# One run of score matmuls for each second-half head, over three banks of PSUM

## The chip, the cores and the metric

The kernel runs on one core of one Trainium2 chip. The metric is the device time of one execution in microseconds (us), as the median of several runs. The engines are TensorE (PE in the profile; its weight loads are PEld), VectorE (DVE), ScalarE (ACT), GpSimd (POOL) and SyncE (SP), which issues all the DMAs of this kernel.

## What is computed

A decayed causal attention over 4 batches of 8 heads, 576 positions and 64 dimensions each, and behind it a mixture of four two-layer experts over the 2304 rows that come out.

```python
scores = q @ k.T / sqrt(D) + (cum[:, None] - cum[None, :])   # cum: running sum of log f
scores = where(causal, -1e9, scores); scores -= max(scores)
attn = exp(scores); attn /= attn.sum() + 1e-9
x = (attn @ v) -> [2304, 512]
for e in range(4):
    out += p[:, e] * (relu(x @ w1[e]) @ w2[e])                # p: normalized domain_probs
```

## The kernel before, in words

A number is held as two parts, a high one and the rest (hi and lo), and a product is three matmuls, or two where one operand carries both parts. The rows of a batch are cut into a first half (queries 0 to 255) and a second half (256 to 575); a job is a pair of heads of one batch and one half, so there are 16 jobs and 32 heads of the second half. This document counts these heads from 0 to 31; the first head of a job is even (`hh` 0), the second odd.

A second-half head has three tiles of 128 queries, tiles 2, 3 and 4, which start at query 256, 384 and 448 (`TOK0`; tile 4 overlaps tile 3 by 64) and see 384, 512 and 576 keys. `qk_pe` (line 600) makes the scores of a tile with two fp32 matmuls for each piece, the first with the high parts (`s<-hi` in the profile), the second with the rests and the decay rows (`s<-kl,q`). A piece is at most one bank of PSUM, 512 columns; tile 4 is cut into two of 288, which take a bank each. `qk_min` (628) adds the mask and takes the minimum of the negated scores on VectorE, out of PSUM into the tile `p`. `qk_exp` (644) does the exponential and its sum on ScalarE. `qk_tile` (656) calls the three in turn for one tile. Behind a head's three tiles `recip16` (673) takes the reciprocals of the sums, and `turn16` (694) splits the probabilities into the two fp16 parts `z` (ScalarE and VectorE) and has SP issue a transposing DMA of each tile into `pt` (726). `av_pair` (806) multiplies a job's `pt` by v for both heads, 28 matmuls into one bank, and `out16` (869) copies the result to its chunk of x on ScalarE. The banks of `ps_a` (four, line 107) hold the scores, the product, and some small transposes.

Interleaved with it, all the time, run the experts: a `Step` (997) has 24 matmuls of the first layer (`l1`, line 1013), a gate on ScalarE and VectorE (1026, 1027), 12 matmuls of the second layer (`l2`, 1046), and every second step a gather of its two output banks on VectorE (`acc`, 1068 and 1073). The weights stream in through SP.

What sets the order: `head_steps` (888) writes for each head a list of small steps with a cost each; `pace` (1552) walks the list so that the sum of costs goes up in a straight line with the experts' steps, in eighths of a step, towards the points at which a chunk of x has to be there, and the end. In this list a second-half head is its tiles (cost `TOK0[t] + 328`: 584, 712, 776), `recip16` and `turn16` at no cost. In an odd head `av_pair` of the job before (cost 1000), `out16` and the steps that make a finished chunk ready stand behind the second entry (line 913). In the first two heads the end of the first half's last job stands behind the first entry (line 919). The order of the list is a priority: within it the framework's planner, which times the kernel by a model, writes down for each engine what it finds ready, and each engine then runs its own order strictly.

Of the kernel before, what the change touches and what calls it, by code (L numbers as in the profile page):

```python
# [8 lines left out]
F32 = mybir.dt.float32  # L9
# [15 lines left out]
TOK0 = (0, 128, 256, 384, 448)  # L25
# [54 lines left out]
def fused(ctx: ExitStack, tc: tile.TileContext, qk, v, f, probs, w, out):  # L80
    nc = tc.nc
# [25 lines left out]
    ps_a = PS("ps_a", 4)  # L107
# [5 lines left out]
    q2 = [once_p.tile([66, S - CH], F32R, name=f"q2_{hh}") for hh in range(2)]  # L113
# [380 lines left out]
    class Job:  # L494
# [96 lines left out]
        def begin(self, hh):  # L591
# [3 lines left out]
            if hh == 0:  # L595
                n = len(self.its)
                self.ssum = st_p.tile([128, 2, n], F32, tag="ssum", name=f"ss{self.nm}")
                self.rs = st_p.tile([128, 2, n], F32, tag="rs", name=f"rs{self.nm}")

        def qk_pe(self, hh, its):  # L600

            at = 512
            for t in its:
                o = self.qo + TOK0[t] - self.q0
                w_ = TOK0[t] + 128
                cuts = ((0, w_),) if w_ <= 512 else ((0, w_ // 2), (w_ // 2, w_))
                for n, (a, z) in enumerate(cuts):
                    if at + z - a > 512:
                        ps = ps_a.tile([128, 512], F32, tag="a", name=f"s{self.nm}_{hh}_{t}_{n}")
                        at = 0  # L610
                    i = TOK0[t] - self.q0
                    for m, (lhsT, rhs) in enumerate(
                        (
                            (self.hi[hh][:, o : o + 128], self.hi[hh][:, self.ko + a : self.ko + z]),
                            (q2[hh][:, i : i + 128], self.kl[hh][:66, a:z]),
                        )
                    ):
                        nc.tensor.matmul(  # L618
                            out=ps[:, at : at + z - a],
                            lhsT=lhsT,  # L620
                            rhs=rhs,
                            start=(m == 0),
                            stop=(m == 1),
                        )
                    self.sp.setdefault((hh, t), []).append((a, z, ps[:, at : at + z - a]))
                    at += z - a

        def qk_min(self, hh, t):
            pt, nm, col = self.p[hh, t], self.nmax[hh], 2 * (t - self.its[0])
# [258 lines left out]
    def head_steps(n):  # L888
# [4 lines left out]
        if n + 1 < len(heads):  # L893
            j, hh = heads[n + 1]
            st.append((0, lambda j=j, hh=hh: j.prep(hh)))
        if n + 2 < len(heads):
            j, hh = heads[n + 2]
            st.append((0, lambda j=j, hh=hh: j.far(hh)))
            st.append((0, lambda j=j, hh=hh: j.load(hh)))
        qs, ts, us = [], [], []  # L900
        if n < len(heads):
            j, hh = heads[n]
            for t in j.its:
                qs.append((TOK0[t] + 328, lambda j=j, hh=hh, t=t: j.qk_tile(hh, t)))
            if j.half:
                qs.append((0, lambda j=j, hh=hh: j.recip16(hh)))
                for t in j.its:
                    qs.append((0, lambda j=j, hh=hh, t=t: j.turn16(hh, t)))
            elif hh == 1:
                qs.append((0, j.recip))  # L910
        if n - 2 >= FIRST and heads[n - 2][1] == 1 and heads[n - 2][0].half:
            j = heads[n - 2][0]
            qs[2:2] = [(1000, j.av_pair), (0, j.out16)] + ready(n - 2)
        if n - 2 >= FIRST and heads[n - 2][0].half == 0:
            j, hh = heads[n - 2]
            late_ = [(200, lambda j=j, hh=hh: j.av(hh))]
# [3 lines left out]
        if FIRST < n <= len(heads):  # L920
            j, hh = heads[n - 1]
            for gi in range(len(j.blocks())):
                ts.append((500, lambda j=j, hh=hh, gi=gi: j.tr(hh, gi)))
        if n + 1 < len(heads):
            j, hh = heads[n + 1]
# [572 lines left out]
    def ready(n):  # L1498
        return [(0, c) for c in sorted(done_at) if done_at[c] == n]
# [3 lines left out]
    for n in range(FIRST, len(heads) + 2):  # L1503
        for cost_, f_ in head_steps(n):
            if type(f_) is int:
                if f_ < LAST[0]:
                    asteps.extend(turn(f_))
                need[f_] = len(asteps)
            else:
                asteps.append((cost_, f_))  # L1510
# [20 lines left out]
    at = 0  # L1531
# [82 lines left out]
    j = heads[FIRST][0]  # L1614
# [159 lines left out]
```

## Time and profile before

| | us |
|---|---|
| median of 3 runs (924.88 to 925.85) | 925.6 |
| the profiled execution | 930.58 |
| span of its instructions | 928.8 |
| TensorE busy in it | 882.4 |
| VectorE busy | 710.0 |
| ScalarE busy | 569.3 |
| GpSimd busy | 528.0 |

The granted TensorE clock was 0.991 of full speed over the span. In the profile an engine is busy from the start of an instruction to its modelled end; matmuls overlap, so the time that one costs is read from the start of one to the start of the next. L618 is line 618. A wait names what ended it.

### The profile page before, as it was taken

What the parts mean: (1) busy time and instruction counts of PE and PEld (TensorE: products, weight loads), DVE (VectorE), ACT (ScalarE), POOL (GpSimd) and SP (SyncE); (2) the same over time, 40 slices, a digit from 0 to 9 for tenths busy, and PEclk for the clock granted to TensorE, in tenths of its full rate; (3) what the DMA queues carried; (4) which work ended last, traced back from release to release, by engine and by line L of the source; (5) the groups of instructions that cost most, each with busy time, mean ns of one, the idle gap of its engine ahead of it and who ended that gap; (6) DMA issues with size and microseconds to landing.
All of it is one profiled execution on the core that took longest, in us unless ns stands there. A gap on an engine that the chain in (4) does not pass through costs nothing.

```text
span 928.8 us, 16629 instructions
## 1 busy us (share of the span) xinstructions
PE 882.4 (95%) x5783; PEld 620.7 (67%) x5783; DVE 710.0 (76%) x1458; ACT 569.3 (61%) x1137; POOL 528.0 (57%) x528
## 2 busy tenths in 40 slices
PE   4899989998998899999999999899998999999998
PEld 3699879898876567666666666554455654666547
DVE  5768766686998888799888887676678647786487
ACT  5868766557676567767767775555665345653350
POOL 4655675655555552455635673785778527885060
PEclk9999989999999999999999999999999999999999
DMA  7457755455979969889999996744323324232003
GB/s 266 144 165 260 260 176 151 159 166 166 262 186 220 283 166 246 219 168 255 265 261 214 262 229 167 246 172 148 115 69 103 125 68 136 68 116 67 23 1 92
DMA packets 147508, 159.45 MB, mean 172 GB/s; under 512 B 86148, under 2 KB 107328, under 8 KB 147424
## 3 DMA queue, kind: packets, MB, share of 16 engines
q1 hardware_dynamic: 147424, 158.39, 61.1%
q8 instruction: 45, 0.74, 0.3%
q14 instruction: 39, 0.32, 0.1%
HBM read 117.30 MB, written 21.65 MB: 150 GB/s over the span
## 4 chain that ended last, share of the span: by engine, by line
PE 55%; POOL 12%; DVE 10%; ACT 7%; DMA 7%; issue 4%; SPq 0%; ACTq 0%; POOLq 0%; DVEq 0%
PE l L1046 16%; PE l L1013 15%; PE y L1284 8%; PE m L1284 7%; PE s L618 4%; POOL s L1344 4%; POOL wt L1178 3%; PE o L818 2%; POOL wu L1178 1%; DMA wr<-in_w 1%; DMA pk<-in_w 1%; DVE acc L1073 1%; DVE z L717 1%; DMA vr<-in_v 1%; ACT wt L1205 1%
## 5 line engine op out<-in xcount | busy, mean ns | idle before, releaser
L1013 PE MATMUL l<-y,w 128*128 128x256 f16 x1248 | 154.8, 275 | 2.7 <-ACT w L980 1.9
L647 ACT ACTIVATE p<-p,nm 128x576 f32<-128x576 f32 (+3 forms) x160 | 95.7, 599 | 82.7 <-DVE nm L632 77.9
L1013 PEld LDWEIGHTS <-w 128*128 128x128 f16 x1248 | 118.4, 99 | 34.2 <-issue 7.1
L1046 PE MATMUL l<-w,gh 128*128 128x512 f16 x408 | 122.2, 382 | 2.7 <-DVE acc L1073 2.0
L564 POOL CAST q<-raw 64x320 fp32r<-64x320 f32 (+1 forms) x56 | 28.1, 502 | 149.6 <-PE s L618 148.2
L1073 DVE SCALAR_TENSOR_TENSOR acc<-y,scg,acc 128x256 f32<-128x256 f32 (+1 forms) x164 | 81.1, 515 | 14.9 <-PE y L1284 14.7
L717 DVE SCALAR_TENSOR_TENSOR z<-p,rs,z 128x384 f16<-128x384 f32 (+3 forms) x128 | 82.4, 665 | 12.7 <-ACT z L716 11.3
L1284 PE MATMUL m<-rh,bs 128*128 128x512 f16 x256 | 86.6, 379 | 0.0
L572 POOL TENSOR_TENSOR kl<-raw,hi 64x576 fp32r<-64x576 f32 (+1 forms) x56 | 66.5, 1188 | 33.8 <-ACT hi L563 28.3
L618 PE MATMUL s<-hi 128*128 128x384 f32 (+1 forms) x192 | 74.9, 394 | 11.3 <-DVE hi L578 8.9
L632 DVE CUSTOM_DVE_ANT_0 p<-s,mask 128x288 f32<-128x288 f32 (+2 forms) x160 | 74.4, 473 | 13.3 <-PE s L618 12.7
L1210 POOL TENSOR_TENSOR bs<-wt,bs 128x512 f16<-128x512 f32 x32 | 38.1, 1192 | 71.3 <-ACT bs L1209 71.1
L1046 PE MATMUL l<-w,gl 128*128 128x512 f16 x204 | 77.3, 382 | 0.0
L716 ACT ACTIVATE z<-p,rs 128x384 f16<-128x384 f32 (+3 forms) x128 | 69.4, 589 | 7.0 <-DVE rs L678 3.4
L1027 DVE SCALAR_TENSOR_TENSOR gl<-l,gh 128x512 f16<-128x512 f32 (+1 forms) x80 | 54.8, 685 | 16.5 <-ACT gh L1026 15.8
L1013 PE MATMUL l<-xh,wh 128*128 128x256 f32 x224 | 65.1, 293 | 0.9 <-ACT xh L859 0.9
L957 POOL TENSOR_TENSOR wl<-wr,wh 128x512 fp32r<-128x512 f32 x48 | 61.7, 1313 | 7.3 <-ACT wh L953 3.6
L1284 PE MATMUL m<-rh,bw 128*128 128x512 f16 x191 | 64.4, 379 | 1.4 <-ACT r L1330 1.4
L1013 PE MATMUL l<-xl,wh 128*128 128x256 f32 x224 | 65.3, 292 | 0.0
L618 PE MATMUL s<-kl,q 66*128 66x384 f32 (+1 forms) x192 | 63.2, 334 | 2.2 <-DMA kl<-nc 2.2
L1013 PE MATMUL l<-xh,wl 128*128 128x256 f32 x224 | 65.2, 292 | 0.1
L1284 PEld LDWEIGHTS <-bs 128*128 128x128 f16 x384 | 37.6, 98 | 38.4
(385 smaller groups left out, 2344.0 us busy)
## 6 DMA issues: line engine op xcount, KB each, us to landing
wr<-in_w SPq DMA_DIRECT2D x90, 512.0 KB
pk<-in_w SPq DMA_DIRECT2D x64, 256.0 KB
wd<-w SPq DMA_DIRECT2D x32, 512.0 KB
raw<-in_qk SPq DMA_DIRECT2D x32, 448.0 KB
bw<-wd SPq DMA_DIRECT2D x32, 256.0 KB
bv<-wd SPq DMA_DIRECT2D x32, 256.0 KB
raw<-in_qk SPq DMA_DIRECT2D x24, 256.0 KB
vp<-in_v SPq DMA_DIRECT2D x10, 512.0 KB
```

The lines of the kernel that those rows point to most:

```text
L572: eng.tensor_tensor(out=kl[:64, :wk], in0=r[:64, ko : ko + wk], in1=hi[:64, ko : ko + wk].bitcast(F32), op=ALU.subtract,)
L618: nc.tensor.matmul(out=ps[:, at : at + z - a], lhsT=lhsT, rhs=rhs, start=(m == 0), stop=(m == 1),)
L632: nc.vector.tensor_tensor_reduce(out=pt[:, a:z], in0=ps, in1=mask[:, m0 + a : m0 + z], scale=-0.125, scalar=BIG if n == 0 else nm[:, col : ...
L647: nc.scalar.activation(out=pt[:, :w_], in_=pt[:, :w_], func=AF.Exp, scale=-1.0, bias=self.nmax[hh][:, c : c + 1], accum_out=self.ssum[:, h ...
L716: nc.scalar.activation(out=o[:, 0], in_=x, func=AF.Copy, scale=sc)
L717: nc.vector.scalar_tensor_tensor(out=o[:, 1], in0=x, scalar=sc, in1=o[:, 0], op0=ALU.mult, op1=ALU.subtract)
L957: eng.tensor_tensor(out=wl[n][:, a:z], in0=r[:, a:z], in1=wh[n][:, a:z].bitcast(F32), op=ALU.subtract,)
L1013: nc.tensor.matmul(out=self.l1p[:, fi, :], lhsT=lhsT, rhs=rhs[:, k, :], start=(k == 0 and m == 0), stop=(k == 3 and m == 2),)
L1027: self.last = nc.vector.scalar_tensor_tensor(out=self.gl, in0=self.l1p, scalar=0.0, in1=self.gh.bitcast(F32) if wide else self.gh, op0=ALU ...
L1046: matmul(out=l2[tt], lhsT=lhsT, rhs=rhs, start=(self.ps == 0 and fi == 0 and m == 0), stop=(self.ps == 1 and fi == 1 and m == 2),)
L1073: nc.vector.scalar_tensor_tensor(out=acc[c][:, tt, d0:d1], in0=ps, scalar=sc, in1=acc[c][:, tt, d0:d1], op0=ALU.mult, op1=ALU.add,)
L1284: line.append(nc.tensor.matmul(**args))
```

## The change

All score matmuls of a second-half head are issued in one run (`qk_head`), ahead of its minima and exponentials: tile 2 and the last 128 keys of tile 4 share a bank, tile 3 has one, the first 448 keys of tile 4 have the third. In the list of steps the run has cost 1400 and each tile's minimum and exponential 224. `av_pair` and what follows it now stand behind the third entry of the list, so behind the run and the minima and exponentials of tiles 2 and 3. For the first half's heads `qk_pe` is written in another way and issues what it did.

```diff
--- before.py
+++ after.py
@@ -597,33 +597,38 @@
                 self.ssum = st_p.tile([128, 2, n], F32, tag="ssum", name=f"ss{self.nm}")
                 self.rs = st_p.tile([128, 2, n], F32, tag="rs", name=f"rs{self.nm}")
 
+        def qk_bank(self, hh, t):
+            return ps_a.tile([128, 512], F32, tag="a", name=f"s{self.nm}_{hh}_{t}")
+
+        def qk_piece(self, hh, t, a, z, ps):
+
+            o, i = self.qo + TOK0[t] - self.q0, TOK0[t] - self.q0
+            for m, (lhsT, rhs) in enumerate(
+                (
+                    (self.hi[hh][:, o : o + 128], self.hi[hh][:, self.ko + a : self.ko + z]),
+                    (q2[hh][:, i : i + 128], self.kl[hh][:66, a:z]),
+                )
+            ):
+                nc.tensor.matmul(out=ps, lhsT=lhsT, rhs=rhs, start=(m == 0), stop=(m == 1))
+            self.sp.setdefault((hh, t), []).append((a, z, ps))
+
         def qk_pe(self, hh, its):
 
             at = 512
             for t in its:
-                o = self.qo + TOK0[t] - self.q0
                 w_ = TOK0[t] + 128
-                cuts = ((0, w_),) if w_ <= 512 else ((0, w_ // 2), (w_ // 2, w_))
-                for n, (a, z) in enumerate(cuts):
-                    if at + z - a > 512:
-                        ps = ps_a.tile([128, 512], F32, tag="a", name=f"s{self.nm}_{hh}_{t}_{n}")
-                        at = 0
-                    i = TOK0[t] - self.q0
-                    for m, (lhsT, rhs) in enumerate(
-                        (
-                            (self.hi[hh][:, o : o + 128], self.hi[hh][:, self.ko + a : self.ko + z]),
-                            (q2[hh][:, i : i + 128], self.kl[hh][:66, a:z]),
-                        )
-                    ):
-                        nc.tensor.matmul(
-                            out=ps[:, at : at + z - a],
-                            lhsT=lhsT,
-                            rhs=rhs,
-                            start=(m == 0),
-                            stop=(m == 1),
-                        )
-                    self.sp.setdefault((hh, t), []).append((a, z, ps[:, at : at + z - a]))
-                    at += z - a
+                if at + w_ > 512:
+                    ps, at = self.qk_bank(hh, t), 0
+                self.qk_piece(hh, t, 0, w_, ps[:, at : at + w_])
+                at += w_
+
+        def qk_head(self, hh):
+
+            two, three, four = (self.qk_bank(hh, t) for t in (2, 3, 4))
+            self.qk_piece(hh, 2, 0, 384, two[:, :384])
+            self.qk_piece(hh, 4, 448, 576, two[:, 384:])
+            self.qk_piece(hh, 3, 0, 512, three)
+            self.qk_piece(hh, 4, 0, 448, four[:, :448])
 
         def qk_min(self, hh, t):
             pt, nm, col = self.p[hh, t], self.nmax[hh], 2 * (t - self.its[0])
@@ -900,8 +905,13 @@
         qs, ts, us = [], [], []
         if n < len(heads):
             j, hh = heads[n]
+            if j.half:
+                qs.append((1400, lambda j=j, hh=hh: j.qk_head(hh)))
             for t in j.its:
-                qs.append((TOK0[t] + 328, lambda j=j, hh=hh, t=t: j.qk_tile(hh, t)))
+                if j.half:
+                    qs.append((224, lambda j=j, hh=hh, t=t: (j.qk_min(hh, t), j.qk_exp(hh, t))))
+                else:
+                    qs.append((TOK0[t] + 328, lambda j=j, hh=hh, t=t: j.qk_tile(hh, t)))
             if j.half:
                 qs.append((0, lambda j=j, hh=hh: j.recip16(hh)))
                 for t in j.its:
@@ -910,7 +920,7 @@
                 qs.append((0, j.recip))
         if n - 2 >= FIRST and heads[n - 2][1] == 1 and heads[n - 2][0].half:
             j = heads[n - 2][0]
-            qs[2:2] = [(1000, j.av_pair), (0, j.out16)] + ready(n - 2)
+            qs[3:3] = [(1000, j.av_pair), (0, j.out16)] + ready(n - 2)
         if n - 2 >= FIRST and heads[n - 2][0].half == 0:
             j, hh = heads[n - 2]
             late_ = [(200, lambda j=j, hh=hh: j.av(hh))]
```

## Rows read from the trace of the kernel before

**Rows 1.** The page, part 1: busy us (share of span) xinstructions

```profile
PE 882.4 (95%) x5783; PEld 620.7 (67%) x5783; DVE 710.0 (76%) x1458; ACT 569.3 (61%) x1137; POOL 528.0 (57%) x528
```

**Rows 2.** Stretches: us, PE, PEld, DVE, ACT, POOL busy, PEclk, DMA share, GB/s

```profile
300.00:325.00 25.00, 22.08 (x156) 14.96 (x154) 21.97 (x48) 15.42 (x33) 12.83 (x13) 0.96 1.08 277
325.00:350.00 25.00, 25.00 (x178) 16.36 (x177) 21.51 (x50) 16.83 (x35) 12.51 (x12) 0.97 0.68 164
...
450.00:475.00 25.00, 25.00 (x185) 17.15 (x184) 21.82 (x50) 17.01 (x36) 13.65 (x12) 1.00 1.08 275
```

**Rows 3.** TensorE's waits: us in total, times, longest

```profile
PE o L818 <- DMA pt<-z: 5.0, 2, 2.7
...
PE l L1046 <- DVE acc L1073: 2.0, 2, 1.6
```

**Rows 4.** TensorE by time: start, us, what [idle before <-releaser]; av_pair's waits

```profile
296.75 1.69 PE L818 MATMUL o<-pt,v 128*64 128x320 f16 x27 [2.75 <-DMA pt<-z]
...
322.14 2.17 PE L818 MATMUL o<-pt,v 128*64 128x320 f16 x27 [2.23 <-DMA pt<-z]
```

**Rows 5.** TensorE by time: runs of tiles 4 and 3, starts of 2

```profile
441.71 0.52 PE L618 MATMUL s<-hi 128*128 128x384 f32 x1
...
447.09 0.38 PE L1046 MATMUL l<-w,gl 128*128 128x512 f16 x1
...
447.84 0.61 PE L1046 MATMUL l<-w,gh 128*128 128x512 f16 x2
...
452.57 0.38 PE L1046 MATMUL l<-w,gl 128*128 128x512 f16 x1
...
453.25 0.61 PE L1046 MATMUL l<-w,gh 128*128 128x512 f16 x2
...
463.30 0.42 PE L618 MATMUL s<-hi 128*128 128x384 f32 x1
```

**Rows 6.** TensorE by time: a pair of 128 columns, first half

```profile
60.76 0.28 PE L1013 MATMUL l<-xl,wh 128*128 128x256 f32 x1
...
61.35 0.22 PE L618 MATMUL s<-hi 128*128 128x128 f32 x1
...
61.69 0.28 PE L1013 MATMUL l<-xl,wh 128*128 128x256 f32 x1
```

**Rows 7.** SP's waits, two transposes on SP, POOL's waits (235 to 575)

```profile
SPq L538 <- PE s L618: 32.0, 21, 6.5
...
288.74 4.57 SPq L726 DMA_TRANSPOSE pt<-z  x2
...
POOL q L564 <- PE s L618: 105.5, 21, 11.0
```

**Rows 8.** VectorE by time, around the end of head 20

```profile
452.24 0.55 DVE L632 CUSTOM_DVE_ANT_0 p<-s,mask 128x384 f32<-128x384 f32 x1
...
453.26 0.43 DVE L675 TENSOR_SCALAR ss<-ss 128x3 f32<-128x3 f32 x1 [0.46 <-ACT p L647]
...
454.58 1.36 DVE L717 SCALAR_TENSOR_TENSOR z<-p,rs,z 128x384 f16<-128x384 f32 x2 [0.68 <-ACT z L716]
```

**Rows 9.** TensorE and VectorE by time: tile 4 of heads 1, 8, 18

```profile
231.40 0.44 PE L618 MATMUL s<-hi 128*128 128x288 f32 x1
...
239.50 0.50 DVE L632 CUSTOM_DVE_ANT_0 p<-s,mask,nm 128x288 f32<-128x288 f32 x1
...
308.81 0.38 PE L618 MATMUL s<-hi 128*128 128x288 f32 x1
...
316.00 0.46 DVE L632 CUSTOM_DVE_ANT_0 p<-s,mask 128x288 f32<-128x288 f32 x1
...
318.73 0.51 DVE L632 CUSTOM_DVE_ANT_0 p<-s,mask,nm 128x288 f32<-128x288 f32 x1
...
425.74 0.38 PE L618 MATMUL s<-hi 128*128 128x288 f32 x1
...
432.12 0.50 DVE L632 CUSTOM_DVE_ANT_0 p<-s,mask,nm 128x288 f32<-128x288 f32 x1
```

## The prediction

> **What bounds the kernel now.** I read the page's busy shares first, then the table of stretches, then TensorE's own waits, then the order on TensorE and VectorE around the scores. The page says that TensorE (PE) is busy for 882.4 of 928.8 us [rows 1]. The second-half heads run through the middle of the span. In its stretches TensorE is full (25.00 of 25 at 450 to 475) or short by a hole that can be named (22.08 at 300 to 325) [rows 2], so whatever adds TensorE time there adds to the end, and whatever closes a hole takes from it. VectorE is busy for about 22 of 25 us there: the second engine in line, not the bound. TensorE's waits in the stage are few [rows 3]: two for the transposed probabilities that the attention-times-v product reads (5.0 us), two for the gather on VectorE (2.0 us in the list). The two big ones stand in the order of time in [rows 4]: 2.75 us before 296.75 and 2.23 us before 322.14, both on the DMA that writes pt. After the second the granted clock falls: 0.96 and 0.97 of full in two stretches that would otherwise show 1.00 [rows 2].
>
> **The change part by part.**
>
> *The matmuls of the scores.* Columns stay at 2944 a head (twice 384, 512 and 576), and matmuls at 8. Three runs become one, and tile 4 is cut into 448 and 128 columns, not 288 and 288. What a run costs above its columns is read from starts, at 2.4 columns a ns. Tile 3: from the fp16 matmul at 452.57 to the next fp16 one at 453.25 is 0.68 us for 512 + 2x512 columns, which are 0.640: 0.040 above. Tile 4: 447.09 to 447.84 is 0.75 for 512 + 4x288, which are 0.693: 0.057 above [rows 5]. Tile 2 also has two matmuls, so it gets 0.040. That is 0.137 us a head. Two runs of 2 and 4 matmuls give 0.0085 us for each matmul and 0.023 for each run. After, six wide matmuls in one run are 0.023 + 6x0.0085 = 0.074.
>
> The two 128-column ones have no row in this stage, but first-half heads have such a pair. From 61.35 to 61.69 a pair of 128 and one of 256 take 0.34 us; 256-column matmuls around them follow each other every 0.118 (60.76 to 61.35 in five steps); so the pair takes 0.222, where its columns are 0.107: 0.115 above [rows 6]. So after is 0.189, and 0.052 more a head: x32 = **+1.7 us**. Bounds: if the narrow pair costs no more than two wide ones (0.017), the term is -1.5; if the run saves nothing (three times 0.023), it is +3.1. I take +1.7, since the narrow rows are of the same operation and the same kind of operands.
>
> [...]
>
> *The place of the attention-times-v product (av_pair).* The list of small steps is paced by its costs. A second-half head costs 584 + 712 + 776 = 2072 before and 1400 + 3x224 = 2072 after, so the pace, which hangs on the list's total and on a chunk that is due before these heads, doesn't change; a pair of heads with its product is 5144 and takes 21.6 us, from one pair's tile 2 at 441.71 to the next one's at 463.30 [rows 5], or 4.2 ns a unit. The product ended 584 + 712 + 1000 = 2296 into its head; it now ends 1400 + 224 + 224 + 1000 = 2848 into it: 2.3 us later. What it waits for (exponentials, the z pieces, their transposes) is tied to the end of the head before last and stays. So 2.75 becomes 0.4 and 2.23 becomes 0: **-4.5 us**. The half-speed stretch behind the second hole costs (0.04 + 0.03) x 25 = 1.75 us [rows 2]; the first, longer hole had none behind it, so I take half: **-0.9 us**. Bounds of this part: 0 (the transposes come later too) and -6.7. Its two ScalarE copies (out16) and the steps that make a chunk ready behind it move with it, still three or more TensorE steps ahead of their use.
>
> *What moves on SP.* No DMA of the head is itself moved against its neighbours, except that scores now end sooner in a head: the small kl load of a later head waits for the last scores, 32.0 us in 21 waits, on SP, with loads, stores and transposes queued behind it [rows 7]; the hole of 2.75 comes after two transposes whose issue took 4.57 us [rows 7]. POOL's copy of q waits for scores too, 105.5 us in this stage [rows 7]. Both shrink; nobody on the path waits for POOL here, so I count nothing.
>
> *Minima and exponentials.* The same instructions, but tile 2 and tile 3 come 1040 and 552 units (4.4 and 2.3 us) later, next to tile 4. They are queued on VectorE and ScalarE ahead of gates and gathers, for which TensorE waits. Before, the next head's tile-2 minimum (0.55 + 0.08 us) fills the time in which VectorE would wait for the last exponential; a wait of 0.46 before the sum's step at 453.26 is left, and another of 0.68 for the first z [rows 8]. The filler now comes later: 0.63 us of VectorE idleness a head. VectorE is at 22 of 25 us in the steady stretch, so a head of 10.8 us has some 1.4 spare and this fits: 0. In the stretches where VectorE lags (7 heads, named below) it is passed on to TensorE: 4.4. I take **+1.0**, nearer to the steady rows.
>
> **The sum.** The profiled run took 930.6 us (span 928.8), 5.0 above the median of 925.6. -4.5 - 0.9 + 1.7 + 1.0 = -2.7 on it: 927.9. Taken over to the median: **922.9 us**. That the timed runs are shorter than the profiled one is a reason to doubt the full 4.5.
>
> **The rivals.**
>
> *The holes are handed on* (about no change). For: the stage is full of near waits, the gather already stops TensorE twice [rows 3], and VectorE's z pieces feed the transposes, so the bunched minima delay what the product waits for. Against: in the steady stretch no such wait shows. If half of the 5.4 is lost, 925.6 - 2.7 + 2.7 = 925.6.
>
> *The three banks make TensorE wait* (slower). The run wants three of four banks at once, and the bank that tile 2 shares with the end of tile 4 is not free until tile 4's first minimum, the other tile-4 bank until its second. The next run comes 1400 units, 5.9 us, after the point at which tile 4 is due. It decides where VectorE is further behind than that. Head 8 is: tile 4's scores start at 308.81, its first minimum at 316.00, its second ends at 319.24 [rows 9], 10.4 us. By the same pairs of rows 7 of the 32 heads are over 5.9 us, from head 1 (231.40 to 240.00) to head 18 (425.74 to 432.63), 14 us above it in all. If the fourth bank is free at that time, only the first minimum counts: two heads, 2.8 us in all. Against: that lag grew partly behind TensorE's own holes. Price between 2.8 and 14; at 7, with the rest as forecast, 922.9 + 7 = 929.9.
>
> *The run isn't one run.* The order on the engines is a planner's, which fills in what is ready; rows of before show fp16 work close around each tile. If it cuts the run by pieces into four, they cost 4x0.040 + (0.115 - 0.017) = 0.258 a head, 0.121 more than before: +3.9, and -5.4 + 3.9 + 1.0 gives 925.1.
>
> **How the numbers follow.** Holes closed, with the surcharge of the narrow pieces: 0.43, at 922.9, its own range 919.5 to 923.7. Handed on: 0.22, at 925.6. Banks: 0.27, at 929.9. Cut up: 0.08, at 925.1. A difference under 0.2%, 1.9 us, can't be told from none. The first case is faster, the second and fourth are the same (0.30), the third is slower. The range takes the best end of the first case short of all its bounds together (918.5) and the banks at somewhat over their middle price (931.5).
>
> **What would show it.** Right: one run of eight fp32 matmuls a head on TensorE; no wait of the product on pt over 0.5 us; full stretches from 275 to 350 and a granted clock of 1.00 there; the interval after a 128-column pair about 0.1 us over its columns. Wrong: waits of the scores' matmuls on VectorE's minima (banks), more wait on the gather (bunched minima), or waits of the product on pt as before (transposes moved too).

## The result: 934.2 us, 0.9% slower

The changed kernel takes 934.17 us (median of 4 runs, 932.07 to 934.77), the kernel before 925.24 beside it: a ratio of 1.0093, with a 95% interval of 1.0075 to 1.011. Two later series gave 1.0122 (1.0083 to 1.0162) and 1.0103 (1.0078 to 1.0128). The forecast was 922.9, its range ended at 931.5.

The page of the changed kernel shows almost nothing of it. Part 1 (busy us, share of the span, instructions), which answers to [rows 1]:

```profile
PE 882.9 (95%) x5783; PEld 622.4 (67%) x5783; DVE 710.0 (76%) x1458; ACT 568.8 (61%) x1137; POOL 528.0 (57%) x528
```

TensorE's waits (us in total, times, longest) answer to [rows 3]:

```profile
PE l L1056 <- DVE acc L1083: 7.1, 6, 3.6
...
PE l L1056 <- ACT gh L1036: 4.4, 4, 3.0
PE l L1056 <- DVE acc L1078: 4.1, 3, 2.2
...
PE l L1023 <- ACT w L990: 2.4, 1, 2.4
...
PE o L823 <- DMA pt<-z: 0.3, 1, 0.3
```

The wait on the transposed probabilities (pt) is gone, as forecast: 0.3 us, after 5.0. But the second layer of the mixture (line 1056, 1046 before) now waits for its gate (L1036) and for the gathers that free its banks (L1078, L1083), and one of these waits alone is 3.6 us. The gate's wait of 3.0 at 227.12 costs little more than what it replaces: at about that point the kernel before has one of 2.7, at 230.66, which the changed kernel lacks (the same view, of before):

```profile
PE topx L200 <- DVE xmax L261: 2.7, 1, 2.7
```

The waits on the gathers, outside of the one of 3.6, add up to 7.6 us, against 2.7 before. No wait of the scores (L612) on a minimum stands in the list: that rival is out. TensorE's stretch from 275 to 350, where the forecast wanted it full, has a clock of 1.00 and 3.6 us of idle time left:

```profile
275.00:350.00 75.00, 71.39 (x535) 49.70 (x534) 67.20 (x146) 51.09 (x104) 33.85 (x34) 1.00 0.94 235
```

**A ruler for the rest.** TensorE's order differs, so times on the clock can't be compared one by one. Two marks can: the first matmul of the mixture's first layer in its step 24 (ahead of nearly all second-half heads), and the 101st matmul of the last stage. What comes behind the second mark takes the same time in all kernels, 293.2 to 293.4 us. Between the marks lies the same work, and the view of stretches splits it; its columns are as in [rows 2]. The kernel before (a second profile of it, see below), first up to step 74 and then the whole:

```profile
219.54:567.12 347.58, 340.20 (x2485) 240.64 (x2484) 304.52 (x675) 249.03 (x503) 183.82 (x163) 0.99 0.94 230
567.12:629.39 62.27, 58.92 (x349) 33.82 (x348) 37.95 (x57) 30.25 (x53) 37.70 (x38) 0.95 0.64 204
219.54:629.39 409.85, 399.12 (x2833) 274.45 (x2832) 342.48 (x731) 279.27 (x555) 221.52 (x200) 0.98 0.89 226
```

The changed kernel, the same three:

```profile
218.54:573.51 354.97, 343.73 (x2487) 245.14 (x2486) 307.25 (x676) 247.96 (x502) 182.37 (x163) 0.99 0.90 227
573.51:639.65 66.14, 58.97 (x349) 33.72 (x348) 36.72 (x54) 30.05 (x52) 40.00 (x37) 0.95 0.55 185
218.54:639.65 421.11, 402.70 (x2835) 278.85 (x2834) 343.97 (x730) 278.01 (x554) 222.36 (x200) 0.98 0.85 220
```

Length less TensorE's busy time is its idle time. Busy time holds some spells at a granted clock of 0.50 (in the changed kernel's trace 512-column fp16 matmuls start 0.427 us apart in them and 0.216 at 1.00, in the median); half of what TensorE works in them is the clock's loss, and busy time less that loss is the work at full speed. For all profiles of this study, in us between the marks:

| kernel | length | idle to step 74 | idle after step 74 | clock's loss | work at full speed |
|---|---|---|---|---|---|
| before, first profile | 411.9 | 10.4 | 3.2 | 5.0 | 393.2 |
| before, second | 409.9 | 7.4 | 3.4 | 6.2 | 393.0 |
| changed, first | 421.1 | 11.2 | 7.2 | 6.4 | 396.3 |
| changed, second | 422.0 | 10.6 | 7.1 | 8.1 | 396.3 |
| changed, third | 421.1 | 12.2 | 7.5 | 4.4 | 397.1 |
| narrow_only | 412.5 | 9.6 | 3.6 | 3.4 | 395.8 |
| av_late_only | 408.3 | 7.1 | 3.4 | 3.0 | 394.8 |
| tail_fix | 415.7 | 9.1 | 4.7 | 4.5 | 397.4 |
| run_four_banks | 418.1 | 12.7 | 6.8 | 6.2 | 392.5 |
| run_minima_spread | 425.7 | 15.8 | 8.1 | 5.0 | 396.7 |
| run_av_old_place | 419.9 | 9.9 | 8.3 | 4.8 | 396.9 |
| narrow_pair_last | 417.4 | 10.6 | 6.5 | 5.8 | 394.5 |
| four_banks_tail | 412.5 | 9.5 | 4.8 | 5.0 | 393.2 |

The mean of the three profiles of the changed kernel is 10.5 us longer than that of the two of before: 3.5 of it is work, 4.0 is idle time after step 74 (the tail), 2.4 is idle time up to step 74, 0.7 is clock. Ahead of the first mark the changed kernel's profiles are 1.2 us shorter in the mean, so the whole executions differ by 9.3. The idle time up to step 74 holds the waits on pt, 3.3 in the mean before and 0.2 after, so the other waits there grew by 5.5. The work of av_late_only, whose matmuls are those of before, came out 1.7 higher, so a single figure of that column is good to somewhat over 1 us.

### The profile page after: what moved, and what is told of

Read it like the earlier page. It is cut to its first block, busy times and chain, and to the rows that moved or that the text cites. A ratio compares the mean times of both kernels' runs of the same rounds, so it can differ in the third digit from the quotient of the medians.

```text
span 933.0 us, 16601 instructions
## 1 busy us (share of the span) xinstructions
PE 882.9 (95%) x5783; PEld 622.4 (67%) x5783; DVE 710.0 (76%) x1458; ACT 568.8 (61%) x1137; POOL 528.0 (57%) x528
## 5 line engine op out<-in xcount | busy, mean ns | idle before, releaser
L1023 PE MATMUL l<-y,w 128*128 128x256 f16 x1248 | 149.1, 274 | 3.2 <-ACT w L990 2.4
L652 ACT ACTIVATE p<-p,nm 128x576 f32<-128x576 f32 (+2 forms) x160 | 95.6, 598 | 84.7 <-DVE nm L637 84.3
L1023 PEld LDWEIGHTS <-w 128*128 128x128 f16 x1248 | 120.9, 98 | 30.6 <-issue 3.4
L1056 PE MATMUL l<-w,gh 128*128 128x512 f16 x408 | 122.0, 382 | 11.2 <-DVE acc L1083 7.1
L722 DVE SCALAR_TENSOR_TENSOR z<-p,rs,z 128x384 f16<-128x384 f32 (+3 forms) x128 | 88.8, 724 | 9.2 <-ACT z L721 8.1
L1083 DVE SCALAR_TENSOR_TENSOR acc<-y,scg,acc 128x256 f32<-128x256 f32 (+1 forms) x164 | 81.1, 515 | 14.9 <-PE y L1294 14.7
L612 PE MATMUL s<-hi 128*128 128x384 f32 (+1 forms) x192 | 68.4, 364 | 11.5 <-DVE hi L578 8.9
L637 DVE CUSTOM_DVE_ANT_0 p<-s,mask 128x128 f32<-128x128 f32 (+1 forms) x160 | 66.2, 441 | 10.3 <-PE s L612 9.6
L1056 PEld LDWEIGHTS <-gh 128*128 128x128 f16 x408 | 37.7, 98 | 49.4 <-issue 15.2
L1023 PE MATMUL l<-xl,wh 128*128 128x256 f32 x224 | 65.2, 292 | 0.0
L612 PE MATMUL s<-kl,q 66*128 66x384 f32 (+1 forms) x192 | 62.3, 340 | 2.4 <-DMA kl<-nc 2.4
```

The lines of the kernel that those rows point to most:

```text
L612: nc.tensor.matmul(out=ps, lhsT=lhsT, rhs=rhs, start=(m == 0), stop=(m == 1))
L637: nc.vector.tensor_tensor_reduce(out=pt[:, a:z], in0=ps, in1=mask[:, m0 + a : m0 + z], scale=-0.125, scalar=BIG if n == 0 else nm[:, col : ...
L652: nc.scalar.activation(out=pt[:, :w_], in_=pt[:, :w_], func=AF.Exp, scale=-1.0, bias=self.nmax[hh][:, c : c + 1], accum_out=self.ssum[:, h ...
L722: nc.vector.scalar_tensor_tensor(out=o[:, 1], in0=x, scalar=sc, in1=o[:, 0], op0=ALU.mult, op1=ALU.subtract)
L1023: nc.tensor.matmul(out=self.l1p[:, fi, :], lhsT=lhsT, rhs=rhs[:, k, :], start=(k == 0 and m == 0), stop=(k == 3 and m == 2),)
L1056: matmul(out=l2[tt], lhsT=lhsT, rhs=rhs, start=(self.ps == 0 and fi == 0 and m == 0), stop=(self.ps == 1 and fi == 1 and m == 2),)
```

## The experiments

**1. The kernel before, profiled again (before_again).** No edit.

> The kernel before, unchanged, for a second profile. The first profile stood 5.0 us above the median of its runs. If that excess was an accident of its first half (the wait of 3.2 us at 125.60 and the half clock from 125.2 to 132.0), the new profile stands within 1.5 us of the median 925.2, has neither, and its tail from the step at about 600 us on is as long as in the first. If the excess is part of the kernel and merely split in another way, the half clock turns up elsewhere and the time is again near 930.

It took 924.57 us, 6.0 less than the first profile. TensorE's waits of this run, beside [rows 3]:

```profile
PE o L818 <- DMA pt<-z: 1.6, 2, 1.0
PE l L1046 <- ACT gh L1026: 1.3, 3, 0.7
PE t L744 <- DVE pt L761: 1.2, 1, 1.2
```

and the product's two waits by time, beside [rows 4]:

```profile
291.70 1.69 PE L818 MATMUL o<-pt,v 128*64 128x320 f16 x27 [0.54 <-DMA pt<-z]
...
315.93 0.87 PE L818 MATMUL o<-pt,v 128*64 128x320 f16 x10 [1.05 <-DMA pt<-z]
```

The same program in the same order: 2.75 and 2.23 us in one execution, 0.54 and 1.05 in another. The wait of 1.2 on L744 was 3.2 in the first profile. These differences, 3.4 on the product and 2.0 on L744, are not the whole account: by the ruler 4.1 of the 6.0 us lie ahead of the first mark, where L744 stands, and only 2.0 between the marks, where the product's waits stand (3.0 less idle time, 1.2 more loss by the clock). What is shown is that two thirds of the waits that the forecast wanted to save are absent from an execution near the median. A stretch at half clock near 125 did stand in this profile too, 3.4 us long where the first had 6.8, and another of 3.4 near 48, so the expectation of none was wrong there.

**2. The narrow cut alone (narrow_only),** on the kernel before:

```diff
-                cuts = ((0, w_),) if w_ <= 512 else ((0, w_ // 2), (w_ // 2, w_))
+                cuts = ((0, w_),) if w_ <= 512 else ((0, 448), (448, w_))
```

> The kernel before with one edit: tile 4 of every second-half head cut at 448 and 128 columns in place of 288 and 288. Order, banks and minima as before. If the narrow pair is what the changed kernel loses on TensorE, the bare time of a head rises by about 0.08 to 0.11 us (two matmuls of about 0.111 us each where their 128 columns alone cost 0.053), 32 heads, +2.5 to +3.5 us, and the minima of unequal pieces cost nothing: 927.7 to 928.8. Rival: the narrow pair's extra is hidden in idle time of TensorE, and the loss is all in the order of the work: 924.5 to 926.0. Rival: a different cut changes what the pieces of the planner's order wait for, and the time moves by over 4 us in either direction.

Measured: 927.01 us, ratio 1.0019 (1.0002 to 1.0036), or 1.8 us more (0.2 to 3.3); the work between the marks is up by 2.7. That is between the range expected (927.7 to 928.8) and the first rival's (924.5 to 926.0). What a run of score matmuls costs above its columns (its excess, from here on) is the time from the start of the matmul ahead of it to the start of the one behind it, less the columns of the one ahead and of the run at 2.4 a ns (in the trace of the kernel before, at a clock of 1.00, 512-column fp16 matmuls start 0.216 us apart and 256-column ones 0.109, in the median: 0.107 us for 256 columns more). Tile 4's run has 0.108 us here and 0.063 with two pieces of 288 (medians of 26 and 25 heads): it costs 0.045 more, less than the 0.1 us a head expected. Summed over all score matmuls of the second half the excess is 7.4 us here and 5.4 in both profiles of the kernel before. What is special is that the narrow pair comes last in its run here. Experiment 7 takes that up. The product is at its old place in this kernel, and its waits on pt are 0.2 us in all.

**3. The later product alone (av_late_only),** on the kernel before: a no-op of 552 units is put in ahead of tile 4 in every second head, whose own cost falls to 224, and the product moves behind it.

```diff
+                late_av = t == 4 and hh == 1 and n - 2 >= FIRST and heads[n - 2][0].half
+                if late_av:
+                    qs.append((552, lambda: None))
+                c_ = 224 if late_av else TOK0[t] + 328
+                qs.append((c_, lambda j=j, hh=hh, t=t: j.qk_tile(hh, t)))
...
-            qs[2:2] = [(1000, j.av_pair), (0, j.out16)] + ready(n - 2)
+            qs[3:3] = [(1000, j.av_pair), (0, j.out16)] + ready(n - 2)
```

> The kernel before with one edit: the pair of attention-times-v products of the second half is placed 552 planner units (about 0.23 us each 552 at full rate) later in its step, behind the place of tile 4, as the changed kernel has it; scores, cuts, banks and minima as before. The prediction's step: the two waits on the transposed probabilities (2.75 and 2.23 us) go and about 5.4 us are gained with the clock behind them: 919.8 to 921. Theory after the result: the waits on the probabilities go, but the holes are handed on to the second layer's wait for the gathered rows, as in the changed kernel (pt waits 5.0 to 0.3, gather waits up by 4.9): 924 to 926. Rival: being later costs by itself, because the row sums that follow come later too: above 927.

(552 units are 2.3 us by the prediction's 4.2 ns a unit; 0.23 us is what 552 columns take.)

Measured: 925.77 us, ratio 1.0004 (0.9986 to 1.0023). No wait on the transposes by DMA is left in the list of TensorE's waits, and the time is the same. The gain of 5.4 us is refuted; what there was to gain, 1.6 us in an execution like the second profile, is under what this interval tells. Whether it was handed on or just too small to see stays open. The gather waits were 2.8 here (1.7 and 1.1) and 2.7 in the second profile of before. But waits on the gate's second part (gl) came up, 1.6 us against 0.3, one of them within the product:

```profile
293.24 0.39 PE L1050 MATMUL l<-w,gl 128*128 128x512 f16 x1 [0.76 <-DVE gl L1031]
```

The idle time up to step 74 is 7.1 us, after 7.4 in that profile, so handing on isn't excluded.

**4. The tail (tail_fix).** The long wait of the changed kernel stands near the end of the mixture's steps. TensorE by time:

```profile
611.79 0.93 PE L1023 MATMUL l<-y,w 128*128 128x256 f16 x7
616.30 1.01 PE L1056 MATMUL l<-w,gh 128*128 128x512 f16 x2 [3.58 <-DVE acc L1083]
```

ScalarE ahead of it:

```profile
608.61 0.72 ACT L1174 ACTIVATE rh<-rx,xsc 128x512 f16<-128x512 f32 x1
610.57 0.72 ACT L1174 ACTIVATE rh<-rx,xsc 128x512 f16<-128x512 f32 x1 [1.24 <-POOL rx L1173]
612.52 0.72 ACT L1174 ACTIVATE rh<-rx,xsc 128x512 f16<-128x512 f32 x1 [1.23 <-POOL rx L1173]
613.15 0.58 ACT L1036 ACTIVATE gh<-l 128x512 f16<-128x512 f32 x1
```

The gate (L1036) stands in ScalarE's queue behind three pieces of the last stage's input (L1174). The second and third wait 1.24 and 1.23 us for GpSimd, and they come one every 1.96 us. ScalarE is idle between them while the gate stands behind; the last matmul of the gate's first-layer sum was done at about 607.5. Then follow gl on VectorE at 614.91 and the gather at 615.51, which frees the bank. In the kernel before the planner put this gate ahead of the four pieces (L1026 and L1164 there):

```profile
607.84 0.58 ACT L1026 ACTIVATE gh<-l 128x512 f16<-128x512 f32 x1
...
609.11 0.72 ACT L1164 ACTIVATE rh<-rx,xsc 128x512 f16<-128x512 f32 x1 [0.20 <-POOL rx L1163]
611.07 0.72 ACT L1164 ACTIVATE rh<-rx,xsc 128x512 f16<-128x512 f32 x1 [1.24 <-POOL rx L1163]
```

None of these instructions is in the diff; what the diff changes in the list stands ahead of them. Every kernel here that has the run is idle for 4.7 to 8.3 us after step 74, every one without it for 3.2 to 3.6, with the product early or late. So the run's entries move the planner's order there; which of their traits does it (costs, number, length) is not shown. In the stretch behind the wait the granted clock was 0.50 of full, after 0.99 from 612.70 to 616.10:

```profile
616.10:619.50 3.40, 3.20 (x8) 1.16 (x8) 2.66 (x5) 0.10 (x1) 3.40 (x5) 0.50 0.83 294
```

The edit on the changed kernel holds these four pieces back and issues them in the last step, behind the previous step's gate:

```diff
+    held = []
...
-            asteps.append((300, lambda k=k, i=i, a_=a_, z_=z_, op=op: x_piece(i, k, op, a_, z_)))
+            f_ = lambda k=k, i=i, a_=a_, z_=z_, op=op: x_piece(i, k, op, a_, z_)
+            asteps.append((300, f_ if i == 0 else lambda f_=f_: held.append(f_)))
...
+        if n == len(steps) - 1:
+            assert len(held) == 4
+            with tc.issue_after(prev.first.ins), tc.issue_after(prev.last.ins):
+                for f_ in held:
+                    f_()
```

> The changed kernel with one edit: the last four pieces of the next input's split (the second block's) are held back until the planner's last step and follow the gate of the step before it on each engine's queue, so that ScalarE meets that gate ahead of them. If the tail theory is right (ScalarE reaches the late gate at 613 us only since it stands behind three such pieces that come every 1.96 us; TensorE then stands 3.58 us and runs 3.4 us at half clock), both go: 5.0 to 5.3 us less than the changed kernel, a ratio to the kernel before of about 1.004 (929). Rival: the end is bounded by the input pieces' own chain on GpSimd and VectorE, so that holding them back puts the same wait a few us later: 933 to 935, ratio 1.009. Rival: the held pieces land in the last matmuls' way and it gets worse: above 936.

ScalarE and TensorE after that edit:

```profile
607.82 0.59 ACT L1036 ACTIVATE gh<-l 128x512 f16<-128x512 f32 x1
...
612.91 0.59 PE L1056 MATMUL l<-w,gh 128*128 128x512 f16 x2 [0.69 <-DVE acc L1083]
```

The gate runs some 5 us earlier, the wait is 0.69 instead of 3.58, and from 612.2 to 619.2 the clock is 1.00. After step 74 the length is 62.8 us, against 66.1, 66.3 and 65.2 in the changed kernel's profiles: about 3.1 less, where 5.0 to 5.3 were expected, since some of it turned into smaller waits (0.5 at 618.38). Of the idle time after step 74, 4.7 us are left, where the changed kernel has 7.3 and the kernel before 3.3: the gate's place is 2.6 of the tail's 4.0. The time is 933.51 us, a ratio of 1.0087 (1.0059 to 1.0115). It doesn't tell this kernel from the changed one and falls into the first rival's range, though the profile shows no wait of that size put back. What the repair is worth in time is not shown by this run alone; experiment 8 has it together with another.

**5. Four banks (run_four_banks).** The changed kernel with the run over four banks and no narrow piece:

```diff
-            two, three, four = (self.qk_bank(hh, t) for t in (2, 3, 4))
+            two, three, four, five = (self.qk_bank(hh, t) for t in (2, 3, 4, 5))
...
-            self.qk_piece(hh, 4, 448, 576, two[:, 384:])
...
-            self.qk_piece(hh, 4, 0, 448, four[:, :448])
+            self.qk_piece(hh, 4, 0, 288, four[:, :288])
+            self.qk_piece(hh, 4, 288, 576, five[:, :288])
```

> The changed kernel with one edit: the run of a head goes over four banks with pieces of 384, 512, 288 and 288 columns, so that no matmul has 128 columns; order of the parts, minima, exponentials and the place of the products as in the changed kernel. Theory: what the narrow pair costs comes back (two matmuls of 128 columns cost about 0.115 us a head over their columns; narrow pair in the kernel before cost 3.3 us by one profile's steps), so 2.0 to 3.3 us less than the changed kernel, and the tail stays as it is, as ScalarE's queue has the late gate behind three pieces in this kernel too: ratio 1.006 to 1.008. Rival: the run itself costs it, not the narrow pair: ratio as the changed kernel's. Rival: a fourth bank makes TensorE wait for banks: waits of the scores on minima appear and it is slower than the changed kernel.

Measured: 932.53 us, ratio 1.0087 (1.0061 to 1.0113), 5.4 us below the changed kernel's 937.91 of the same series, whose interval (1.0083 to 1.0162) overlaps with this one. The range expected ended at 1.008. So the time alone does not settle it; the matmuls in the profile do. One head's run, from its first matmul to the first behind it, in the changed kernel:

```profile
492.90 0.42 PE L612 MATMUL s<-hi 128*128 128x384 f32 x1
493.17 0.34 PE L612 MATMUL s<-kl,q 66*128 66x384 f32 x1
493.35 0.22 PE L612 MATMUL s<-hi 128*128 128x128 f32 x1
493.41 0.28 PE L612 MATMUL s<-kl,q 66*128 66x128 f32 x1
493.52 0.44 PE L612 MATMUL s<-hi 128*128 128x512 f32 x1
493.80 0.40 PE L612 MATMUL s<-kl,q 66*128 66x512 f32 x1
494.04 0.37 PE L612 MATMUL s<-hi 128*128 128x448 f32 x1
494.24 0.37 PE L612 MATMUL s<-kl,q 66*128 66x448 f32 x1
494.46 0.72 PE L1023 MATMUL l<-y,w 128*128 128x256 f16 x5
```

and with four banks:

```profile
495.70 0.42 PE L612 MATMUL s<-hi 128*128 128x384 f32 x1
495.96 0.34 PE L612 MATMUL s<-kl,q 66*128 66x384 f32 x1
496.14 0.40 PE L612 MATMUL s<-hi 128*128 128x512 f32 x1
496.37 0.40 PE L612 MATMUL s<-kl,q 66*128 66x512 f32 x1
...
497.15 0.83 PE L1023 MATMUL l<-y,w 128*128 128x256 f16 x6
```

1.56 us against 1.45 for the same 2944 columns. The excess of a whole run is 0.246 us in the changed kernel and 0.139 with four banks (medians of 23 and 20 heads), 0.107 less; by 32 heads 3.4 us. Summed over all score matmuls of the second half it is 8.6 to 8.8 us in the three profiles of the changed kernel, 5.4 here and 5.4 in the kernel before. The work between the marks falls by 4.1 (from 396.6 in the mean to 392.5). The rows show where it lies: the second narrow matmul's successor starts 0.11 us behind it, where its columns take 0.053, and the one after, of 512 columns, takes 0.28 (493.52 to 493.80), where the same matmul takes 0.23 without a narrow one ahead. The first narrow matmul's successor starts 0.06 behind it. What makes the narrow matmuls dear is not shown. The weight loads (PEld) don't tell; one of this run by time, and the group of fp16 loads in the page's part 5 (columns: busy, mean ns of one, idle before):

```profile
493.35 0.19 PEld L612 LDWEIGHTS s<-kl,q 66*128 66x128 f32 x1
...
L1023 PEld LDWEIGHTS <-w 128*128 128x128 f16 x1248 | 120.9, 98 | 30.6 <-issue 3.4
```

An fp32 load is 0.19 us long in the profile, about twice the 98 ns of an fp16 one. But the load shown ends at 493.54, and the matmul that uses it starts before that, at 493.41, so these rows show no wait of a matmul for its load. The run itself saves nearly nothing: 392.5 against 393.1 of the kernel before, which has three runs a head. No wait of the scores on a minimum appeared, so four banks were not too few. The tail was as in the changed kernel, as expected (6.8 us idle, the wait before 618.21 is 3.00); the idle time up to step 74 was the largest but one, which ate part of the gain.

**6. The bunched minima (run_minima_spread, run_av_old_place).** On the changed kernel, the first edit gives the run a cost of 400 and the minima costs of 184, 712 and 776, which puts tile 3's and tile 4's minima and exponentials and the product back at the places of before:

```diff
-                qs.append((1400, lambda j=j, hh=hh: j.qk_head(hh)))
+                qs.append((400, lambda j=j, hh=hh: j.qk_head(hh)))
...
-                    qs.append((224, lambda j=j, hh=hh, t=t: (j.qk_min(hh, t), j.qk_exp(hh, t))))
+                    qs.append(({2: 184, 3: 712, 4: 776}[t], lambda j=j, hh=hh, t=t: (j.qk_min(hh, t), j.qk_exp(hh, t))))
```

> The changed kernel with one edit: the minima and exponentials of tiles 3 and 4 of a second-half head stand at the places in the step where the kernel before has them (after 584, 1296 and 2072 planner units), and with them the pair of products; the run of eight matmuls stays whole at the step's start. Theory of the handed-on holes: gather waits between 300 and 540 come from the minima that stand bunched in VectorE's queue ahead of the gathers; spread out, these waits fall from 5 to 7 us to 2 or 3 and the kernel is 3 to 4 us faster than the changed one. Its late gate stands behind four pieces, so the tail's wait of 3 us or more stays: ratio 1.004 to 1.007. Rival: the bunching costs nothing and the gather waits are the order's accidents: ratio as the changed kernel's, within 0.2%.

The second moves only the product:

```diff
-            qs[3:3] = [(1000, j.av_pair), (0, j.out16)] + ready(n - 2)
+            qs[1:1] = [(1000, j.av_pair), (0, j.out16)] + ready(n - 2)
```

> The changed kernel with one edit: the pair of products stands two places earlier, at the place that the kernel before has for it; run and bunched minima stay. The prediction's step: then the waits on the transposed probabilities return, some 5 us. Theory after the second profile of before, which had 1.6 us of them instead of 5.0: they return as 0.5 to 2 us only, and vary from one execution to the next, since it is a transfer that is waited for.

Spreading made it worse: 939.68 us, ratio 1.0154 (1.0125 to 1.0184), with 15.8 us idle up to step 74. The gather waits there are 5.4 us, where 2 to 3 were expected and the changed kernel's three profiles have 7.6, 6.0 and 8.5; waits on gl, 0.2 to 1.1 us in the changed kernel, came to 5.2. It is no clean test of the place alone: with a cost of 400 for a run that takes as long as before the planner's due times are wrong by 1000 units around each head. So it neither confirms the theory nor rules it out. With the product alone back, 1400 units into its head where it was 1296 before, one run gave 933.89 us; the only wait on pt is 0.22 us, less than the 0.5 to 2 expected, so it did not return. In this kernel the minima stay bunched, and the gather waits are 3.1 us only, near the 2.7 of the kernel before; the gate's waits grew from 3.0 to 6.2 instead. So bunched minima alone don't make the gather waits. In both, the tail changed again. TensorE at the start of the last stage, with the minima spread:

```profile
599.39 0.39 PE L1296 MATMUL m<-rh,bw 128*128 128x512 f16 x1 [4.40 <-ACT rh L1174]
...
602.51 0.59 PE L1294 MATMUL m<-rl,bw 128*128 128x512 f16 x1 [2.73 <-DVE rl L1175]
```

(4.54 and 2.53 with the product at its old place.) Here it is the last stage that waits for its input pieces, and 8.1 and 8.3 us are idle after step 74.

**7. The narrow pair last (narrow_pair_last),** with the changed kernel's time in the same series (after_third) and its second profile from an earlier one (after_again):

```diff
-            self.qk_piece(hh, 4, 448, 576, two[:, 384:])
             self.qk_piece(hh, 3, 0, 512, three)
             self.qk_piece(hh, 4, 0, 448, four[:, :448])
+            self.qk_piece(hh, 4, 448, 576, two[:, 384:])
```

> The changed kernel with one edit: the pair of 128-column matmuls comes last in the run instead of between tile 2 and tile 3; same banks, same pieces. The excess of a head's run over its columns was 0.224 us with the pair in the middle, 0.116 without it (four banks), and in the kernel before, where only the cut was changed and the pair came last of four, 0.096 against 0.049. Theory: a narrow matmul is dear where the next weights are those of a wide one in fp32; last in the run only one of the two is, so the excess falls to about 0.165, 32 heads: 1.5 to 2.0 us less than the changed kernel. Rival: place does not matter: 0.22 as before and the same time.

> The changed kernel, unchanged, once more: its time in the same series as the two that follow. Theory as it stands: 3.4 us of the loss are matmul time (the stretch from step 24 to the hundredth matmul of the last stage, with waits and half clock taken out, is 396.5 us in two profiles of the changed kernel and 393.1 in two of the kernel before), 3.8 us are the tail, and the rest is waits in the middle: ratio 1.009 to 1.012.

> The changed kernel, unchanged, for a second profile and for its time beside the kernel before in the same series as the three that follow. If the loss is in the order of the work and in the matmuls, which are fixed in the program, the second profile shows the same long waits: about 3.0 us at 224, 3.6 us before 616 behind the gate of ScalarE, gather waits of together 5 to 7 us between 300 and 540, and no wait on the transposed probabilities over 0.5 us; ratio 1.008 to 1.011. If the 3.6 us in the tail was an accident of one execution, as the 3.2 us of the first profile of before were, it is not there.

The changed kernel gave 933.46 us (1.0103, 1.0078 to 1.0128) and before that 937.91 (1.0122, 1.0083 to 1.0162). Its waits stood in the same places all three times: 3.03 us of the gate before the second layer near 227 to 230, 3.58, 3.43 and 3.42 in the tail, 0.29, 0.16 and 0.23 on pt. So they belong to the program and not to an execution. The waits on gathers outside that tail add up to 7.6, 6.0 and 8.5 us by the lists of waits, against 2.7 in both profiles of the kernel before.

With the pair last: 930.99 us, ratio 1.0073 (1.0047 to 1.0099), 2.5 us below the changed kernel beside it, with intervals that overlap. One head's run:

```profile
503.55 0.42 PE L612 MATMUL s<-hi 128*128 128x384 f32 x1
...
504.87 0.22 PE L612 MATMUL s<-hi 128*128 128x128 f32 x1
504.93 0.28 PE L612 MATMUL s<-kl,q 66*128 66x128 f32 x1
505.04 0.83 PE L1023 MATMUL l<-y,w 128*128 128x256 f16 x6
```

1.49 us. The excess of a run is 0.193 us in the median of 21 heads, 0.053 below that with the pair in the middle (0.246) and 0.054 above that without the pair (0.139). The expectation, whose figures take the ends of a run in another way, wanted 0.059 less. The sum over all score matmuls of the second half is 7.0 us, after 8.6 to 8.8, and work falls by 2.1 us between the marks. So the place counts: the pair costs 0.107 us in the middle of the run and 0.054 at its end, where fp16 matmuls follow. That the type of the next weights is the reason is not shown.

**8. Both repairs (four_banks_tail):** the edits of experiments 4 and 5 together.

> The changed kernel with both repairs: four banks without a 128-column matmul, and the last four pieces of the input's split behind the late gate. If the two causes are separate and add up, the matmul time falls by 3.4 to 4 us and the tail by 3.5: 7 to 7.5 us less than the changed kernel, ratio to the kernel before 1.001 to 1.004, and what is left are the waits in the middle (2 to 5 us more than the kernel before). Rival: what is taken away in one place comes back as waits in another, as with the four banks alone, where the waits in the middle grew by 1.5 us: 1.005 or more.

Measured: 929.05 us, ratio 1.0048 (1.0025 to 1.007), 4.4 us below the changed kernel of the same series. Between the marks the profile lost 8.9 us: 3.4 of work and 2.4 of idle time in the tail, as the two repairs promise, and 1.9 of idle time up to step 74 and 1.3 of clock, which no edit was made for. The timed gain is smaller than the 7 to 7.5 expected, and the ratio lies between the range given (1.001 to 1.004) and the rival's (1.005 or more), with an interval that reaches into both. In the profile the two causes add up; in time the two repairs together are clear of the changed kernel beside them (its interval is 1.0078 to 1.0128), but neither is by itself: four banks alone have 1.0061 to 1.0113, the tail's repair alone 1.0059 to 1.0115. By the interval 2.3 to 6.5 us of the loss remain. No version of this study beats the kernel before.

## Why the prediction was wrong, step by step

*The base and the product's place (-5.4): wrong, and this is the step that failed first.* The product comes later, and the waits on pt are down to 0.2 to 0.3 us in every profile of the changed kernel. That the later place took them away is not shown: with the product at its old place, narrow_only and run_av_old_place have 0.2 us of them as well. The gain was not there. The step read 2.75 and 2.23 us [rows 4] in one execution that stood 5.0 above the median, computed 927.9 for that execution, and then took the whole difference over to the median. Experiment 1 shows that an execution near the median has 1.6 us of these waits, and experiment 3 that moving the product alone gives 1.0004. The forecast named this doubt in its own sum ("a reason to doubt the full 4.5") and did not act on it: with 1.6 for 5.0 and no clock the sum would have been +1.1, not -2.7. That would still have been 926.3, so the rest of the miss lies in the other terms.

*The scores' matmuls (+1.7): right in sign, half in size.* The narrow pair was sized well from a row of another stage [rows 6]: 0.098 above two wide ones, measured 0.107. What failed is the saving of the longer run: 0.046 us a head, or 1.5 us, from a split into a part for each run and one for each matmul that two rows [rows 5] could not carry. Four banks show no saving: an excess of 5.4 us for all heads, as before. So the term was +3.3 by these sums and +3.5 by the ruler, just above its bound of +3.1. The reading of 0.222 us for the pair [rows 6], 0.111 for each of its matmuls, was an average: the rows of the changed kernel show 0.06 us from the first one to its successor and 0.11 from the second, and 0.05 more behind the matmul after the pair.

*Bunched minima (+1.0): too small, and the cause is not confirmed.* Idle time up to step 74 other than on pt grew by 5.5 us, from 5.6 in the mean of two profiles to 11.1 in that of three, above the term's upper end of 4.4. Most of it stands on the gathers, as the forecast's own sign of being wrong had it. But the cause given is not borne out: with the minima still bunched and the product early the gather waits are 3.1 us (experiment 6). What makes these waits is open. Kernels with the same order there differ by 3 us from one execution to the next (12.7 with four banks, 9.5 with four banks and the tail's repair), so a single profile can't settle it.

*The tail: not in the forecast at all.* It is 4.0 us more idle time in the mean of three profiles that agree within 0.4, with a stretch at half clock behind the longest wait in two of them, in a stretch where no score is computed any more. The forecast said that the pace "doesn't change" since a head's costs sum to 2072 as before. The sum was right, the conclusion was not: the order changed up to the end, and there a gate came to stand behind pieces that wait for GpSimd. Experiment 4 shows it by putting the gate back, which takes 2.6 of the 4.0 away. That it is the size of the single entries that moved the planner is the likely reason and was not tested.

*The rivals.* "Handed on" was closest in kind, since new waits on the gathers stand in the middle where those on pt are gone, but neither the place nor the size was that of the forecast. "Banks" had the time nearest to the result, 929.9, and its mechanism is refuted: no score waits for a minimum in the changed kernel. "Cut up" happens in 9 of 32 heads. The heads with a whole run show the added 0.107 us as well, so the cutting isn't what costs that; a cut head has some 0.08 us more, 0.7 us for the nine.

## What to carry to other kernels

Profile the kernel before twice before a gain is read from its waits: waits on a transfer that are 5.0 us in one execution and 1.6 in another are no term of a sum made for a median. An edit in a list that a planner orders moves instructions that the diff doesn't touch, so look for the place where a short instruction could come to stand in an engine's queue behind slow, waiting ones (here a gate of 0.58 us behind three pieces, ahead of a wait of 3.58 us on TensorE), and count that as a rival. A pair of narrow fp32 matmuls cost twice as much in the middle of its run as at its end here (0.107 us and 0.054): put it last, or cut the columns evenly.

## What the runs showed of the hardware

The same program, with the same order on every queue, waited 2.75 and 2.23 us on the same two transposes in one execution and 0.54 and 1.05 in another, and timed runs of the kernel before spread from 920.7 to 929.5 us in one series. A narrow fp32 pair cost 0.107 us a head in the middle of a run and 0.054 at the end of it, more than two wide ones. One run of eight matmuls between fp16 work, with four banks, cost no less than runs of two, two and four: 5.4 us above the columns over 32 heads in both cases. Which wait has a stretch at half clock behind it differed between executions: the longest wait in the tail was followed by one in two of three profiles of the changed kernel (behind 3.58 and 3.43 us), and in the third, behind 3.42 us, by none.
